# A gated attention scan and a spatial gating unit on one core: a re-timed plan, wider filler matmuls, and the last output tiles in the weight space

## The chip, the cores and the metric

The kernel runs on one core of a Trainium2 chip. The metric is the device time of one execution in microseconds. Five engines work side by side: TensorE (PE in the profile; its weight loads are PEld), VectorE (DVE), ScalarE (ACT), GpSimd (POOL) and SyncE (SP), which here only issues DMAs. Each has its own queue and runs it strictly in order; semaphores tie the queues together.

## The reference, cut to what matters

```python
# q, k, v, alpha: (4, 8, 768, 48)
for t in range(S):                       # S = 768
    state = alpha[:, :, t, :, None] * state + einsum('bhd,bhe->bhde', k[:, :, t], v[:, :, t])
    y[:, :, t] = einsum('bhd,bhde->bhe', q[:, :, t], state)
x = y.transpose(0, 2, 1, 3).reshape(4, 768, 384)
h = maximum(x @ w_in, 0)                 # (4, 768, 1024)
u, v = h[..., :512], h[..., 512:]
v_n = (v - mean(v)) / sqrt(var(v) + 1e-6)
v_s = einsum('ts,bsd->btd', w_spatial, v_n) + b_spatial[None, :, None]
out = (u * v_s) @ w_out                  # (4, 768, 384), float32
```

## The kernel before, in words

**First part, the scan.** Each of the four batches has six chunks of 128 time steps, so there are 24 chunks, 0 to 23. Chunks 0 to 5 go in pairs (`pair`, `PAIRS`), the others singly (`first`). For a chunk, SP loads alpha, k, q and v (`ac`, `kc`, `qc`, `vc`). ACT takes logarithms (`ln`), PE sums them up over time (`cum`), ACT takes exponentials (`einv`, `eexp`, `ebc`). POOL or DVE scales k (`kt`), DVE scales q (`qt`), PE transposes both (`tr`, `trk`), and an evacuation `ev` copies them to `kqT`. PE computes scores (`sc`) into two banks, DVE masks each (`m`, tile `ptm`), and PE forms the chunk's output `y` from the masked scores, v (`vb`) and the state of the chunk before. The state is carried by `upd` (PE), `z` (DVE, L327 and L329), `S` (L334) and `sb` (L209, a copy in two halves into `sbd`). The output is copied (`xs`), transposed (`xt`) and copied into the batch's `xT` (`xe`).

**Second part, per batch.** `second_v` computes the gate half of h for a tile of 128 rows, with its statistics: on DVE (`bn`, L837 and L838), or, for the pairs of tiles named in `ACT_STATS`, on ACT with three small DVE operations `mv` after it. Then come `rs` (ACT) and `vn` (DVE). `second_u` computes the other half, transposed (`uT`). `second_s` multiplies by the spatial weights, adds the bias on DVE (`vsb`, L915) and multiplies by u on POOL (`gT`, L928). `second_o` multiplies by `w_out`, copies a tile of 128 x 384 out of PSUM and stores it. There are 24 such output tiles, numbered n = 6 x batch + row tile. Names such as s-3-0-1 give batch, column slice and row half; o-3-2 is row tile 2 of batch 3.

**The order of work is a plan.** All of this is first written down as operations with a cost on each engine that may run them, with dependencies, a priority and a patience. `schedule` (L96) then places one after the other: at each step the operation and engine with the earliest start, where `PATIENCE` moves the start that is compared, and it emits the instruction. The costs are constants in the code (`ENGINES`, and the numbers in calls of `op`), as are the assumed times of loads (`LD`, and `lat` in `dma`, 1.9 us). The plan so fixes, ahead of time, the order of every engine's queue and on which engine an operation lies. At run time only semaphores decide when an instruction starts.

**Junk matmuls.** While the planned time is below `WARM` = 40 us, `schedule` fills the time for which PE is planned to be idle with matmuls on a constant tile `junk`, in pieces of at most 192 columns. `bank` (L194) emits them, into the bank that the next real operation will overwrite. They do no work of the reference.

**Output tiles.** Where `out_tile` (L935) puts a tile depends on n. Tiles 0 to 7 lie in two tiles of the pool `raws` (`raw_w`, four output tiles each), through which the weights were loaded earlier. Tiles 8 to 10 lie in `w_row`, also of that pool. All the others rotate through four buffers of `outp` (`o_sb`), so that tile n needs the store of tile n - 4 to have landed. The stores stand in SP's queue behind all the loads.

Of the kernel before, what the change touches and what calls it, by code (L numbers as in the profile page):

```python
# [51 lines left out]
class Clock:  # L52
# [19 lines left out]
        return end  # L72


PATIENCE = {"ev": -0.3, "v": -0.1, "g": -0.3, "sb": 0.3, "bb": 0.5, "ln": 0.2, "z": -0.2, "we": -0.1, "S": 0.2, "cast": -0.1, "rs": 0.1, "trk": -0.1, "xs": -0.3}
ENGINES = {
    "kt": {"POOL": 0.87},
    "vb": {"POOL": 0.47, "ACT": 0.42},
    "S": {"POOL": 0.57},
    "sb": {"POOL": 0.79, "DVE": 0.36},  # L80
    "vn": {"DVE": 0.33},
    "xe": {"ACT": 0.38},
    "ev": {"DVE": 0.61, "ACT": 0.91},
    "u": {"ACT": 0.38, "DVE": 0.47},
    "o": {"ACT": 0.38},
}
PAIRS = (0, 1, 2)
ACT_STATS = ((2, 2), (1, 4), (3, 4))
PIECES = {
    "w_in": ((0, "vc", 0, 0.35), (0, "kc", 2, 0.15)),  # L90
    "w_sp": ((0, "vc", 4, 0.35), (0, "qc", 6, 0.25), (0, "qc", 6, 0.25)),
    "w_out": (0, "qc", 7, 0.25),
}
# [2 lines left out]
def schedule(ops, fill, warm_from, warm_to):  # L96

    free = {}
    clock = Clock()
    todo = list(ops)  # L100
    while todo:
        best = None
        for n, op in enumerate(todo):
            if any(d.end is None for d in op.deps):
                continue
            ready = max([d.end + d.lat for d in op.deps], default=0.0)
            waits = [slot.ring.free_at(k) for k, slot in enumerate(op.take)]
            if None in waits:
                continue
            ready = max([ready] + waits)  # L110
            for eng, dur in op.eng.items():
                start = max(ready, free.get(eng, 0.0))
                key = (round(start + (0.5 * dur if len(op.eng) > 1 else 0.0) + op.wait, 2),
                       ready if eng == "DMA" else op.prio)
                if best is None or key < best[0]:
                    best = (key, n, eng, start, dur)
        assert best is not None, "nothing can start"
        _, n, eng, start, dur = best
        op = todo.pop(n)
        if eng == "PE":  # L120
            if op.take and start < warm_to:
                t = max([free.get(eng, 0.0), warm_from] + [slot.ring.free_at(k) for k, slot in enumerate(op.take)])
                while True:
                    each = 0.00042 if clock.warm(t) else 0.00084
                    cols = min(192, int((start - t) / each) // 32 * 32)
                    if cols < 96:
                        break
                    fill.append(cols)
                    t = clock.run(t, 0.00042 * cols, cols)
            end = clock.run(start, dur, op.cols)  # L130
        else:
            end = start + dur
        for slot in op.take:
            slot.ring.taken.append(slot)
        free[eng] = end
        op.end = end
        op.emit(eng)
# [3 lines left out]
def kernel(  # L141
# [31 lines left out]
    IO = 3  # L173
    WK = 3
    NB, NKP = 3, 2
    LD, LP, WT, ST = 0.97, 1.46, 2.35, 0.8
    NRAW, NROW, KEEP = 2, 3, 11
    raws = ctx.enter_context(tc.tile_pool(name="raws", bufs=NRAW))
    io_pool = ctx.enter_context(tc.tile_pool(name="io", bufs=IO))
# [14 lines left out]
    def bank(pool, shape, dtype, **kw):  # L194

        t = pool.tile(shape, dtype, **kw)
        flat = t if len(shape) == 2 else t.rearrange("p a b -> p (a b)")
        for cols in fill:
            nc.tensor.matmul(out=flat[:, 0:cols], lhsT=junk[:, 0:128], rhs=junk[:, 0:cols], start=True, stop=True)  # L199
        fill.clear()  # L200
        return t

# [15 lines left out]
    ut_ones = consts.tile([128, 128], BF16, name="ut_ones")  # L218
    ident = consts.tile([128, 128], BF16, name="ident")
    mask4 = consts.tile([128, 4, 128], BF16, name="mask4")  # L220
    junk = consts.tile([128, 192], BF16, name="junk")
    ones_row = consts.tile([1, 128], BF16, name="ones_row")
    ones_col = consts.tile([128, 1], BF16, name="ones_col")
    eps_tile = consts.tile([128, 1], FP32, name="eps_tile")
# [66 lines left out]
    def op(key, *args, **kw):  # L291

        users = kw.pop("use", ())
        o = Op(*args, **kw)
        for s in users:
            s.users.append(o)
        ops.append(o)
        made[key] = o
        o.wait = PATIENCE.get(key[0], 0.0)
        return o  # L300

    def got(*keys):
        return [made.get(x) for x in keys]
# [86 lines left out]
    def pair(j):  # L390
# [33 lines left out]
        for par in range(2):  # L424
# [42 lines left out]
                    out=ktp[:, par, :, :, 0:D].rearrange("p hp s d -> p (hp s) d"),  # L467
                    in0=st["kc"][:, :, par, :], in1=st[f"binv{par}"])

            op(("ktp", j, par), {"POOL": 0.87, "DVE": 0.47}, None, ktf, got(("einvp", j, par), ("kc", 2 * j)) + tr_users("k", jo), prio=P + 4)  # L470

            def qtf(_, par=par):
                nc.vector.tensor_mul(
# [116 lines left out]
    def first(i):  # L590
# [13 lines left out]

        j = i // 2
        jo = j - NKP
        dma(("ac", i), LD, load("ac", alpha), io_users("ln", j), P)
        dma(("kc", i), LD, load("kc", k), io_users("kt", j), P + 0.1)
        dma(("qc", i), LD, load("qc", q), io_users("qt", j), P + 0.2)
        dma(("vc", i), LD, load("vc", v), io_users("vb", j), P + 0.3)  # L610

        la, kt, qt = [x[j % NKP][:, i % 2].rearrange("p (hp s) d -> p hp s d", s=2) for x in (lap_bufs, ktp_bufs, qtp_bufs)]

# [196 lines left out]
    def second_v(b, tt):  # L810
# [33 lines left out]
        if on_act:  # L844
            def mv(_):
                d = bt[b]
                nc.vector.tensor_scalar_mul(out=d["mvs"][:, two, 0], in0=d["sums"][:, 0, two], scalar1=1.0 / DH)
                nc.vector.tensor_tensor(
                    out=d["mvs"][:, two, 1], in0=d["mvs"][:, two, 0], in1=d["mvs"][:, two, 0], op=ALU.mult)
                nc.vector.scalar_tensor_tensor(  # L850
                    out=d["mvs"][:, two, 1], in0=d["sums"][:, 1, two], scalar=1.0 / DH, in1=d["mvs"][:, two, 1],
                    op0=ALU.mult, op1=ALU.subtract)

            op(("mv", b, t0), "DVE", 0.4, mv, got(("bn", b, t0), ("bn", b, tt)), prio=6.0)

        def rs(_):
            d = bt[b]
# [38 lines left out]
    def second_s(b, dsl, th):  # L896
        last = b == B - 1 and dsl == NDS - 1 and th == 1
        mms = []
        if last:
            mms.append(mm(  # L900
                lambda ps: ps[:, 0:TH], lambda: ones_row, lambda: b_sp_sb[:, th * TH:(th + 1) * TH], True, False))
        for st in range(NT):
            mms.append(mm(
                lambda ps: ps[:, 0:TH], lambda st=st: bt[b]["vn"][:, st, dsl * 128:(dsl + 1) * 128],
                lambda st=st: w_spT[:, st, th * TH:(th + 1) * TH], st == 0 and not last, st == NT - 1))
        hold = {}
        cols = slice(th * TH, (th + 1) * TH)

        def evac(eng, ps):
            if last:  # L910
                nc.vector.tensor_tensor(
                    out=bt[b]["gT"][:, dsl, cols], in0=ps[:, 0:TH], in1=bt[b]["uT"][:, dsl, cols], op=ALU.mult)
            else:
                hold["vs"] = small.tile([128, TH], FP32, name="vsb", bufs=4)
                nc.vector.tensor_tensor(out=hold["vs"], in0=ps[:, 0:TH], in1=bsp_bc[:, th, :], op=ALU.add)  # L915

        Q = 1000.0 + 100 * b + 20 + th * NDS + dsl
        us = got(("u", b, dsl, th))
        pdeps = [[made[("vn", b, t)] for t in tt] for tt in ((0, 1, 2, 3), (4, 5))]
        us = us + got(*[("we", 3 * th + t) for t in range(3)])  # L920
        group(("s", b, dsl, th), mms, 0.165, [made[("v", b, t)] for t in range(NT)] + us,
              Q, evac, "DVE", 0.47,
              us + got(("be", th)) + [made.get(("o", b - 2, x)) for x in range(NT)], parts=2, pdeps=pdeps)
        if last:
            made[("g", b, dsl, th)] = made[("s", b, dsl, th)]
        else:
            def gm(eng):
                ENG[eng].tensor_tensor(  # L928
                    out=bt[b]["gT"][:, dsl, cols], in0=hold["vs"], in1=bt[b]["uT"][:, dsl, cols], op=ALU.mult)

            op(("g", b, dsl, th), {"POOL": 0.87} if b < B - 1 else {"POOL": 0.87, "DVE": 0.46}, None, gm, got(("s", b, dsl, th)), prio=Q)

    kept = {}

    def out_tile(n):  # L935

        if n < 8:
            if n % 4 == 0:
                kept["t"] = raws.tile([128, 4 * DM], FP32, name="raw_w")
            return kept["t"][:, n % 4 * DM:(n % 4 + 1) * DM]  # L940
        if n < KEEP:
            return raws.tile([128, S], BF16, name="w_row", bufs=NROW).bitcast(FP32)
        return outp.tile([128, DM], FP32, name="o_sb")

    def second_o(b, tt):
# [5 lines left out]
        if n < 8:  # L951
            free = [made[("cast", "w_out", x)] for x in range(NDS)] + [made[("cast", "w_sp", 2, x)] for x in range(2)]
        elif n < KEEP:
            free = got(("wt", n - 8 + 3))
        else:
            free = got(("st", (n - 4) // NT, (n - 4) % NT)) if n >= KEEP + 4 else []

        def evac(eng, ps):
            hold["o"] = out_tile(n)
            copy(eng, hold["o"], ps[:, 0:DM])  # L960

        Q = 1000.0 + 100 * b + 30 + tt
        group(("o", b, tt), mms, 0.165, [made[("g", b, x, tt // 3)] for x in range(NDS)] + made[("w_out",)], Q, evac,
# [113 lines left out]
```

## Time and profile before

| | us |
|---|---|
| median of 5 runs | 155.53 |
| lowest, highest | 155.25, 156.05 |
| profiled execution, own time | 155.52 |
| its span, first to last instruction | 153.66 |

The span is 1.9 us shorter than the execution's own time. In the profile, each engine's busy time is given beside its share of the span. "Idle before, releaser" is the time for which an engine stood still just before an instruction, and what ended that. "issue" as a releaser means that nothing that the profile shows was waited for. The bar of a matmul is drawn with the time that it takes to go through the array, so bars of matmuls in sequence overlap; the distance from start to start tells the pace. In strings of digits, each digit is the busy share of one fortieth of the span in tenths.

### The profile page before, as it was taken

Reading aid. Unit: us, or ns where it says so; the run is one execution under the profiler, and the core shown is the slowest. Engines: PE = TensorE matmul, PEld = TensorE weight load, DVE = VectorE, ACT = ScalarE, POOL = GpSimd, SP = SyncE. Lnnn points to the kernel's source line nnn. Section 1 sums busy time; section 2 is a strip of 40 time slices with the busy share of each in tenths; the row PEclk is TensorE's granted clock in tenths of the full one; section 3 lists DMA queues with packets and bytes.
Section 4 is the critical chain, followed back from the end, with each engine's and each line's share of the span. In section 5 each row is a group of like instructions: output and inputs, shape, how many; then the busy total and the mean of one; then the engine's idle time right before and its main releaser. Section 6 shows DMA issues by size and latency. Waiting matters only on the chain.

```text
span 153.7 us, 4564 instructions
## 1 busy us (share of the span) xinstructions
PE 143.7 (94%) x1746; PEld 95.3 (62%) x1761; DVE 123.2 (80%) x268; ACT 111.1 (72%) x273; POOL 84.0 (55%) x141
## 2 busy tenths in 40 slices
PE   7999799999999999999999999999999989999960
PEld 6697567766657556666557575755666646666530
DVE  7666589589999999996888998799979997467900
ACT  3586486899999596899895599999955947860141
POOL 6737247755337888834389498515757851005400
PEclk9999999999999999999999999999999999999998
DMA  4999999998999999989899799899894013400053
GB/s 124 265 314 292 311 211 290 229 281 161 220 232 216 230 182 203 201 164 211 161 215 205 151 201 212 162 216 220 192 376 171 2 51 107 154 0 0 2 196 117
DMA packets 93016, 28.62 MB, mean 186 GB/s; under 512 B 87873, under 2 KB 91457, under 8 KB 92993
## 3 DMA queue, kind: packets, MB, share of 16 engines
q1 hardware_dynamic: 92960, 28.32, 78.4%
q8 instruction: 14, 0.23, 0.7%
q14 instruction: 10, 0.07, 0.1%
q0 software_dynamic: 32, 0.00, 0.0%
HBM read 23.60 MB, written 4.72 MB: 184 GB/s over the span
## 4 chain that ended last, share of the span: by engine, by line
PE 74%; ACT 8%; DVE 5%; DMA 5%; POOL 2%; issue 2%; ACTq 0%; DVEq 0%; POOLq 0%
PE ps L775 41%; PE pt L672 4%; PE pt L702 4%; DMA out_dram<-o_sb 3%; PE y L363 3%; DMA ac<-in_alpha_dram 2%; PE y L730 2%; PE cum L621 2%; PE tp L688 2%; PE y L573 2%; PE ps L199 2%; POOL gT L928 2%; PE ps L430 2%; PE y L724 2%; PE ps L495 2%
## 5 line engine op out<-in xcount | busy, mean ns | idle before, releaser
L775 PE MATMUL ps<-w_spT,vn 128*128 128x384 bf16 x192 | 36.2, 326 | 0.0
L928 POOL TENSOR_TENSOR gT<-vsb,uT 128x384 bf16<-128x384 f32 x28 | 25.8, 930 | 17.3 <-DVE vsb L915 16.9
L713 DVE TENSOR_TENSOR ptm<-pt,mask 128x512 bf16<-128x512 f32 x36 | 23.5, 682 | 2.0 <-PE pt L702 1.8
L775 PEld LDWEIGHTS <-vn 128*128 128x128 bf16 x192 | 17.1, 97 | 10.2 <-issue 0.2
L645 POOL TENSOR_TENSOR kt<-kc,binv 128x384 bf16<-128x384 f32 x18 | 16.5, 920 | 10.5 <-ACT bc L640 5.5
L334 POOL TENSOR_TENSOR state<-state,bc 128x192 f32<-128x192 f32 x20 | 10.3, 513 | 20.3 <-DVE state L329 12.6
L775 PE MATMUL ps<-w_out_sb,gT 128*128 128x384 bf16 x96 | 18.6, 326 | 0.0
L775 PE MATMUL ps<-xT,w_in 128*128 128x384 bf16 x96 | 18.4, 326 | 0.0
L207 ACT CAST x_sb<-y 128x384 bf16<-128x384 f32 x24 | 11.4, 480 | 9.2 <-PE y L730 6.4
L915 DVE TENSOR_TENSOR vsb<-ps,bsp_bc 128x384 f32<-128x384 f32 x31 | 16.3, 550 | 2.1 <-PE ps L775 1.2
L775 PE MATMUL ps<-w_in,xT 128*128 128x512 bf16 x57 | 16.1, 380 | 1.2 <-ACT xT L207 0.2
L207 ACT COPY o_sb<-ps 128x384 f32<-128x384 f32 x13 | 6.2, 476 | 11.3 <-PE ps L775 9.7
L837 DVE BATCH_NORM_STATS2 stats<-v_sb 128x6 f32<-128x512 bf16 x18 | 12.3, 685 | 1.5 <-ACT v_sb L213 1.4
L213 ACT ACTIVATE v_sb<-ps 128x512 bf16<-128x512 f32 x18 | 10.7, 596 | 3.8 <-PE ps L775 3.4
L207 ACT COPY xT<-y 128x384 bf16<-128x384 bf16 x24 | 11.4, 486 | 1.4 <-PE y L363 1.1
L209 POOL CAST sbd<-state 64x192 bf16<-64x192 f32 x30 | 11.2, 374 | 1.3
L199 PEld LDWEIGHTS <-junk 128*128 128x128 bf16 x112 | 10.4, 108 | 2.0 <-DVE junk L240 1.1
L775 PEld LDWEIGHTS <-gT 128*128 128x128 bf16 x96 | 8.4, 97 | 5.0
L775 PEld LDWEIGHTS <-w_in 128*128 128x128 bf16 x96 | 8.4, 97 | 4.9
L215 DVE TENSOR_SCALAR uT<-ps 128x384 bf16<-128x384 f32 x16 | 8.5, 553 | 3.4 <-PE ps L775 3.3
L867 DVE TENSOR_SCALAR vn<-v_sb,mvs,rstd 128x512 bf16<-128x512 bf16 x24 | 10.5, 473 | 0.8 <-ACT rstd L860 0.7
L775 PEld LDWEIGHTS <-xT 128*128 128x128 bf16 x72 | 6.1, 98 | 6.8 <-ACT xT L207 2.4
(128 smaller groups left out, 314.2 us busy)
## 6 DMA issues: line engine op xcount, KB each, us to landing
ac<-in_alpha_dram SPq DMA_DIRECT2D x18, 192.0 KB, 4.1
kc<-in_k_dram SPq DMA_DIRECT2D x18, 192.0 KB, 4.1
qc<-in_q_dram SPq DMA_DIRECT2D x18, 192.0 KB, 3.7
vc<-in_v_dram SPq DMA_DIRECT2D x18, 192.0 KB, 4.1
out_dram<-o_sb SPq DMA_DIRECT2D x13, 192.0 KB, 2.1
raw_w<-in_moe_w_spatial_dram SPq DMA_DIRECT2D x3, 768.0 KB, 6.2
raw_w<-in_moe_w_in_dram SPq DMA_DIRECT2D x2, 768.0 KB, 8.2
out_dram<-raw_w SPq DMA_DIRECT2D x8, 192.0 KB, 2.5
```

Source lines behind the costliest of these rows:

```text
L199: nc.tensor.matmul(out=flat[:, 0:cols], lhsT=junk[:, 0:128], rhs=junk[:, 0:cols], start=True, stop=True)
L207: nc.scalar.copy(out=out, in_=in_)
L209: ENG[eng].tensor_copy(out=out, in_=in_)
L213: nc.scalar.activation(out=out, in_=in_, func=AF.Relu)
L334: ENG[eng].tensor_tensor(out=st["state"], in0=st["state"], in1=st["bc"][:, :, None].to_broadcast([128, HP, D]), op=ALU.mult)
L645: ENG[eng].tensor_mul(out=kt[:, :, :, 0:D], in0=quad(st["kc"]), in1=st["binv"])
L713: nc.vector.tensor_tensor(out=st["ptm"][:, s], in0=st[f"pt{s}"], in1=mask4, op=ALU.mult)
L775: return lambda ps: nc.tensor.matmul(out=out(ps), lhsT=lhsT(), rhs=rhs(), start=start, stop=stop)
L837: nc.vector.bn_stats(out=stats, in_=d["v_sb"][:, tt, :])
L867: nc.vector.tensor_scalar(out=d["vn"][:, t, :], in0=d["v_sb"][:, t, :], scalar1=d["mvs"][:, t, 0:1], scalar2=d["rstd"][:, t:t + 1], op0=AL ...
L915: nc.vector.tensor_tensor(out=hold["vs"], in0=ps[:, 0:TH], in1=bsp_bc[:, th, :], op=ALU.add)
L928: ENG[eng].tensor_tensor(out=bt[b]["gT"][:, dsl, cols], in0=hold["vs"], in1=bt[b]["uT"][:, dsl, cols], op=ALU.mult)
```

## The change

Five things change at once.

- The planner's constants: costs in `ENGINES` and in some calls of `op`, patience, and an assumed load latency `LATE` = 3.5 us for the chunks 6 to 23 in place of 1.9. `S` and `sb` may both run on POOL or DVE. `ACT_STATS` has two pairs of tiles in place of three. One of the two `w_in` loads is tied to the load of v of the second chunk in place of the first, which leaves its place in the queue as it was.
- A table `NUDGE` of 21 single operations, each with a shift of its patience.
- Junk matmuls of up to 384 columns in place of 192, cut to the width of the bank that they are written to; the tile `junk` is 384 columns wide.
- The last four output tiles, n = 20 to 23, lie in one more `raw_w` tile in place of `o_sb`. They depend on the stores of tiles 0 to 3.
- The copy of tile 23 out of PSUM is split in two halves, one on ACT and one on DVE.

With the new constants, the planner gives every engine another order from early on. PE's first 24 groups stay as they are; after that, the first part's chunks 6 to 8 come later among the second part's work. `NUDGE` puts o-3-2 behind o-3-3, o-3-4 and o-3-5 at the very end.

```diff
-PATIENCE = {"ev": -0.3, "v": -0.1, "g": -0.3, "sb": 0.3, "bb": 0.5, "ln": 0.2, "z": -0.2, "we": -0.1, "S": 0.2, "cast": -0.1, "rs": 0.1, "trk": -0.1, "xs": -0.3}
+PATIENCE = {"ev": -0.3, "kt": -0.2, "v": -0.1, "be": 0.2, "sb": 0.3, "bb": 0.2, "ln": 0.2, "z": -0.2, "we": -0.1, "S": 0.2, "cast": -0.1, "rs": 0.1, "trk": -0.1, "xs": -0.3, "xe": -0.2, "y": -0.2}
 ENGINES = {
-    "kt": {"POOL": 0.87},
-    "vb": {"POOL": 0.47, "ACT": 0.42},
-    "S": {"POOL": 0.57},
-    "sb": {"POOL": 0.79, "DVE": 0.36},
-    "vn": {"DVE": 0.33},
-    "xe": {"ACT": 0.38},
+    "kt": {"POOL": 0.9},
+    "vb": {"POOL": 0.48, "ACT": 0.42},
+    "S": {"POOL": 0.5, "DVE": 0.6},
+    "sb": {"POOL": 0.73, "DVE": 0.95},
+    "vn": {"DVE": 0.42},
+    "xe": {"ACT": 0.4},
     "ev": {"DVE": 0.61, "ACT": 0.91},
-    "u": {"ACT": 0.38, "DVE": 0.47},
-    "o": {"ACT": 0.38},
+    "u": {"ACT": 0.39, "DVE": 0.49},
+    "o": {"ACT": 0.4},
+}
+NUDGE = {
+    ("m", 9, 0): -0.15,
+    ("vn", 0, 4): -0.3,
...
+    ("ebc", 0): 0.15,
...
+    ("kc", 0): 1,
+    ("o", 3, 2, "mm", 0): 0.3,
...
 }
 PAIRS = (0, 1, 2)
-ACT_STATS = ((2, 2), (1, 4), (3, 4))
+LATE = 3.5
+ACT_STATS = ((2, 2), (0, 2))
 PIECES = {
-    "w_in": ((0, "vc", 0, 0.35), (0, "kc", 2, 0.15)),
+    "w_in": ((0, "vc", 1, 0.35), (0, "kc", 2, 0.15)),
...
-                    cols = min(192, int((start - t) / each) // 32 * 32)
+                    cols = min(384, int((start - t) / each) // 32 * 32)
...
-    LD, LP, WT, ST = 0.97, 1.46, 2.35, 0.8
+    LD, LP, WT, ST = 1.03, 1.46, 2.35, 0.8
...
         for cols in fill:
-            nc.tensor.matmul(out=flat[:, 0:cols], lhsT=junk[:, 0:128], rhs=junk[:, 0:cols], start=True, stop=True)
+            for c in range(0, cols, flat.shape[1]):
+                n = min(cols - c, flat.shape[1])
+                nc.tensor.matmul(out=flat[:, 0:n], lhsT=junk[:, 0:128], rhs=junk[:, 0:n], start=True, stop=True)
...
-    junk = consts.tile([128, 192], BF16, name="junk")
+    junk = consts.tile([128, 384], BF16, name="junk")
...
-        o.wait = PATIENCE.get(key[0], 0.0)
+        o.wait = PATIENCE.get(key[0], 0.0) + NUDGE.get(key, 0.0)
...
-        dma(("ac", i), LD, load("ac", alpha), io_users("ln", j), P)
+        dma(("ac", i), LD, load("ac", alpha), io_users("ln", j), P, lat=LATE)
...
-            op(("mv", b, t0), "DVE", 0.4, mv, got(("bn", b, t0), ("bn", b, tt)), prio=6.0)
+            op(("mv", b, t0), "DVE", 0.9, mv, got(("bn", b, t0), ("bn", b, tt)), prio=6.0)
...
-            op(("g", b, dsl, th), {"POOL": 0.87} if b < B - 1 else {"POOL": 0.87, "DVE": 0.46}, None, gm, got(("s", b, dsl, th)), prio=Q)
+            op(("g", b, dsl, th), {"POOL": 0.9} if b < B - 1 else {"POOL": 0.9, "DVE": 0.69}, None, gm, got(("s", b, dsl, th)), prio=Q)
...
-        if n < 8:
+        if n < 8 or n >= B * NT - 4:
...
+        elif n >= B * NT - 4:
+            free = got(*[("st", 0, x) for x in range(4)])
...
             hold["o"] = out_tile(n)
-            copy(eng, hold["o"], ps[:, 0:DM])
+            if n < B * NT - 1:
+                copy(eng, hold["o"], ps[:, 0:DM])
+                return
+            half = DM // 2
+            copy("ACT", hold["o"][:, 0:half], ps[:, 0:half])
+            copy("DVE", hold["o"][:, half:DM], ps[:, half:DM])
```

The loads of k, q and v of chunks 6 to 23 get `lat=LATE` in the same way, and the cost of `ktp` goes from 0.87 and 0.47 to 0.9 and 0.6.

More of the change, by code (lines that the diff above doesn't have):

```diff
@@ L72, in run @@
         return end
-PATIENCE = {"ev": -0.3, "v": -0.1, "g": -0.3, "sb": 0.3, "bb": 0.5, "ln": 0.2, "z": -0.2, "we": -0.1, "S": 0.2, "cast": -0.1, "rs": 0.1, "trk": -0.1, "xs": -0.3}
+PATIENCE = {"ev": -0.3, "kt": -0.2, "v": -0.1, "be": 0.2, "sb": 0.3, "bb": 0.2, "ln": 0.2, "z": -0.2, "we": -0.1, "S": 0.2, "cast": -0.1, "rs": 0.1, "trk": -0.1, "xs": -0.3, "xe": -0.2, "y": -0.2}
 ENGINES = {
-    "kt": {"POOL": 0.87},
-    "vb": {"POOL": 0.47, "ACT": 0.42},
-    "S": {"POOL": 0.57},
-    "sb": {"POOL": 0.79, "DVE": 0.36},
-    "vn": {"DVE": 0.33},
-    "xe": {"ACT": 0.38},
-    "ev": {"DVE": 0.61, "ACT": 0.91},
-    "u": {"ACT": 0.38, "DVE": 0.47},
-    "o": {"ACT": 0.38},
+    "kt": {"POOL": 0.9},
[4 more added lines that the diff above has]
+    "xe": {"ACT": 0.4},
+    "ev": {"DVE": 0.61, "ACT": 0.91},
+    "u": {"ACT": 0.39, "DVE": 0.49},
[4 more added lines that the diff above has]
+    ("vn", 0, 4): -0.3,
+    ("qt", 22): -0.3,
+    ("upd", 2): 0.3,
+    ("v", 0, 5): 0.6,
+    ("vbp", 0, 0): -0.6,
+    ("z", 21): 1.5,
+    ("ebc", 0): 0.15,
+    ("ev", "q", 1, 1): 0.15,
+    ("z", 19): -1.5,
+    ("cast", "w_in", 0, 1): -0.15,
+    ("vb", 21): -0.15,
+    ("y", 19): -1.5,
+    ("kc", 0): 1,
+    ("o", 3, 2, "mm", 0): 0.3,
+    ("sc", 1, 0): -0.3,
+    ("tr", "k", 0, 1): -0.3,
+    ("qtp", 0, 0): -0.15,
+    ("y", 2): 0.15,
+    ("xs", 22): -0.3,
+    ("m", 20, 0): 0.6,
 }
 PAIRS = (0, 1, 2)
-ACT_STATS = ((2, 2), (1, 4), (3, 4))
+LATE = 3.5
+ACT_STATS = ((2, 2), (0, 2))
 PIECES = {
-    "w_in": ((0, "vc", 0, 0.35), (0, "kc", 2, 0.15)),
+    "w_in": ((0, "vc", 1, 0.35), (0, "kc", 2, 0.15)),
     "w_sp": ((0, "vc", 4, 0.35), (0, "qc", 6, 0.25), (0, "qc", 6, 0.25)),
@@ L468, in ktf @@
                     in0=st["kc"][:, :, par, :], in1=st[f"binv{par}"])
-            op(("ktp", j, par), {"POOL": 0.87, "DVE": 0.47}, None, ktf, got(("einvp", j, par), ("kc", 2 * j)) + tr_users("k", jo), prio=P + 4)
+            op(("ktp", j, par), {"POOL": 0.9, "DVE": 0.6}, None, ktf, got(("einvp", j, par), ("kc", 2 * j)) + tr_users("k", jo), prio=P + 4)
             def qtf(_, par=par):
@@ L606, in first @@
         jo = j - NKP
-        dma(("ac", i), LD, load("ac", alpha), io_users("ln", j), P)
-        dma(("kc", i), LD, load("kc", k), io_users("kt", j), P + 0.1)
-        dma(("qc", i), LD, load("qc", q), io_users("qt", j), P + 0.2)
-        dma(("vc", i), LD, load("vc", v), io_users("vb", j), P + 0.3)
+        dma(("ac", i), LD, load("ac", alpha), io_users("ln", j), P, lat=LATE)
+        dma(("kc", i), LD, load("kc", k), io_users("kt", j), P + 0.1, lat=LATE)
+        dma(("qc", i), LD, load("qc", q), io_users("qt", j), P + 0.2, lat=LATE)
+        dma(("vc", i), LD, load("vc", v), io_users("vb", j), P + 0.3, lat=LATE)
         la, kt, qt = [x[j % NKP][:, i % 2].rearrange("p (hp s) d -> p hp s d", s=2) for x in (lap_bufs, ktp_bufs, qtp_bufs)]
```

## The prediction

> **What bounds the kernel now.** I read the page's first two parts, then TensorE's idle times, then the chain at the end. The busy shares:
>
> ```profile
> PE 143.7 (94%) x1746; PEld 95.3 (62%) x1761; DVE 123.2 (80%) x268; ACT 111.1 (72%) x273; POOL 84.0 (55%) x141
> ...
> PE   7999799999999999999999999999999989999960
> ```
>
> TensorE (PE) is the bound from 2 us to 148.6 us; nobody else is at nine tenths for so long. But not all of it is work: line L199 is junk, put in to fill idle time that the planner foresees. From start to start a junk matmul of 192 columns takes 83 ns, one real matmul of 384 columns 162 ns. The order of PE's instructions has 112 junk matmuls, 20,896 columns; 4,544 of them run before the first real matmul, while the first load is on its way, and cost nothing. The other 16,352 are 16,352/192 x 83 ns = 7.1 us, all before 39 us. Junk is executed whether PE is late or not, so **what delays PE early on is not made up by it**. A PE delay therefore reaches the end, unless another engine is later still.
>
> Second, what PE waited for:
>
> ```profile
> PE y L573 <- issue: 1.0, 1, 1.0
> PE y L724 <- DVE sbd L209: 0.7, 1, 0.7
> ```
>
> (us in total, times, longest), and at these two places of the timeline (start, us, then in brackets the idle time and its releaser):
>
> ```profile
> 16.94 0.27 PE L573 MATMUL y<-vbp,ptm 64*128 64x48 bf16 x4 [1.01 <-issue]
> ...
> 123.91 0.34 PE L724 MATMUL y<-sbd,kqT 128*128 128x96 bf16 x4 [0.66 <-DVE sbd L209]
> ```
>
> A matmul's bar reaches past the start of the next one, so I count waits from start to start, less the usual pitch. Above 0.25 us and after 5 us that gives: 1.17 us at 15.7 (in the middle of one y, waiting for no engine), 0.46 at 34.8 (chunk 6's transposes `trk`, behind masks on VectorE), 0.39 at 74.6 (v, behind ACT's xT), 0.28 at 78.0 (scores, behind ACT's kqT copy of 1.02 us), 0.83 at 122.9 (y, behind two state copies on DVE, 0.47 and 0.40 us). In all 3.1 us: more can't be got back in the middle.
>
> The first belongs to this row of part 3:
>
> ```profile
> q8 instruction: 14, 0.23, 0.7%
> ```
>
> 14 packets, 0.23 MB, so 16 KB each: PE's instructions (its 3,524 matmuls and weight loads alone are about 14 x 256). One starts at 14.31 us and lasts 1.23 us, among loads that keep the DMA engines full. PE stops after its 452nd matmul or weight load at 15.7 us and goes on at 16.94.
>
> Third, the end:
>
> ```profile
> 145.18 3.41 PE L775 MATMUL ps<-w_out_sb,gT 128*128 128x384 bf16 x20
> ...
> 147.33 0.48 ACT L207 COPY o_sb<-ps 128x384 f32<-128x384 f32 x1 [0.17 <-PE ps L775]
> 149.43 0.94 ACT L207 COPY o_sb<-ps 128x384 f32<-128x384 f32 x2 [1.62 <-DMA out_dram<-o_sb]
> ```
>
> PE is done at 148.59, yet the last two copies wait for a store that frees their buffer: `outp` has four. The last store is issued at 150.40, SP sees the last landing at 152.55, and closing takes 1.1 us, to 153.66.
>
> **What the Trainium skill says.** Runtime: NRT & Kernel Launch, "Instruction fetch mechanics": instructions are refilled in 16 KiB blocks of 256, over DMA, while the current block executes, "mostly hidden". The trace agrees on the size, and shows one block that was not hidden (1.0 us). TensorE: Matmul & The Clock Gate, "Back-to-back issue gap": warm pitch N/2.4 + 2.5 ns, so 162.5 for 384 columns and 82.5 for 192; the trace has 162 and 83. The same page, "What's actually happening": half the clock until about 3.4 us of activity. The first 24 junk matmuls take 3.97 us, 165 ns each, later ones 83. DMA: Bandwidth & Descriptors, "Latency and other measured facts": about 2 us fixed per DMA; stores of o_sb land after 1.8 to 3.9 us, median 2.1.
>
> **The change, part by part.**
>
> *Wider junk.* 71 matmuls in place of 112, 22,752 columns, of which 4,544 are again the free ones. The rest, 18,208, at 162/384 to 83/192 ns a column, are 7.7 to 7.9 us: **+0.7 us** on PE. The extra sits before y-4 (1,376 columns) and v-0-4 (640). If PE would have waited there anyway the price is 0; the full 0.85 us of those two is the other end.
>
> Each piece less is one matmul and one weight load less. PE reaches its 452nd such instruction not at y-1 but ten groups on, where before stood at about 20 us; the 256 instructions up to there take some 8 us in place of 5.5. A block that came 1.2 us late then has 3 us to spare. **-1.0 us**, from 0 (the chains of DVE and ACT take it) to -1.2. I don't take all, as the planner still writes 0.38 to 0.40 us for ACT copies that take 0.48.
>
> The junk tile's memset doubles (0.22 us now); its cover is the 0.3 us that PE then waits for the first logarithm anyway: 0.
>
> *Plan.* New costs, patience and nudges change the order on every queue; arithmetic and loads are the same. Work moves: five state copies `sb` (2 x 0.364 us each on DVE) and seven uT (0.553) leave DVE, one on-ACT statistics pair (1.73 on DVE, less 0.78 for its three small operations) comes, three S (0.35 by the nearest row, the state sum L329; at most the 0.51 that POOL takes), two kqT copies (1.1) come, one kt, one w_spT go: DVE -3.6 -3.9 +1.0 +1.05 +1.1 -1.1 + 0.3 (half a copy) = about -5 us, to 118. ACT -2.1 +3.4 -1.6 -1.0 with small ones: about -1, to 110. POOL +3.7 (sb, 0.75 each) -1.5 +0.9 +1.0 +0.5 = about +4.6, to 89. PE's sum doesn't change. Of the waits, 122.9 goes (its sb is on POOL), 78.0 goes (that copy is on DVE, 0.68 for 1.02), 34.8 goes (trk-6 is twelve groups later): **-1.6 us**. 74.6 stays. POOL's cover is its 45% idle; without it, each sb 0.75 us long would hold up the next y.
>
> The plan takes 3.5 us for a load's latency where 1.9 stood, so chunks 6 to 13 come later, while loads keep SP's order but for a few exchanges: the buffers that they wait for come free later. Loads were ahead of their use by 4 us at chunk 6, which covers that.
>
> What is late next: the masks. A y needs its scores' two masks: 0.16 + 1.28 + 0.06 = 1.5 us after the last score matmul if DVE is free. Adding up PE durations in the new order, the distance is 1.5 to 2.0 us for chunks 7, 10 to 13, 22 and 23, where before only 7 and 8 had less than 2. With one DVE operation of 0.55 ahead of the masks in each, y's would wait 2.2 us in all; with none, 0. I take half. Besides, o-3-2 is nudged to the very end, so only o-3-1 covers the last gT (0.56 us on DVE): 0.25 us. **+1.35 us**, from 0.25 to 2.5.
>
> *Tiles.* The last four output tiles get one `raw_w` tile, whose readers, the first stores, were issued from 115 us on. No copy waits for a store. PE's end aside, the last copy (o-3-2, whole, 0.48 on ACT) ends at 148.59 + 0.04 + 0.48 = 149.11, against 150.37: **-1.25 us**. The halved copy of tile 23 is last but one and wins nothing. Five of the last six SP issues take 0.33 to 0.62 us, one 1.14, so SP is free by then; landing is taken at 2.1. If four stores in flight slow the last to 3.9, it ends 0.5 us later than now; if 1.8, another 0.3 is won.
>
> Sum: 0.7 - 1.0 - 1.6 + 1.35 - 1.25 = -1.8 us. The profiled execution took 155.52 us (span 153.66), the median of the five is 155.53: **153.7 us**.
>
> **Rivals.**
> 1. *The middle gives nothing*: what the fetch and the waits free is lost to DVE and ACT, whose chains run through the same 40 us. For it: DVE is at nine tenths in most slices from 30 us on, ACT in many. Against: DVE loses 5 us of work. Junk +0.7, tail -1.25: 155.0.
> 2. *Late masks make it slower*: the place is y of chunks 7 to 13 and 18 to 23, the price what DVE holds before the masks. With 0.8 us there, they wait 4.5 us: 0.7 - 1.0 - 1.6 + 4.7 - 1.25 = +1.55, 157.1. It decides from about 0.7 us. Against: the same 0.8 would have cost y's 1.3 us before, and none of its waits of 0.15 or more is at those y's but the one behind sbd.
> 3. *The tail's gain is eaten by landing*: 3.9 us, as one store showed at 145.4. -1.8 + 1.25 + 0.5: 155.5.
>
> **How the numbers follow.** The forecast has 0.64, rival 1 0.16, rival 2 0.13, rival 3 0.07. Best ends of the unknown terms (+0.7 - 1.2 - 1.6 + 0.25 - 1.5) give 152.2, worst short of rival 2 about 155.5. Range 152.0 to 155.5; rival 2 lies outside. About 0.3%, 0.47 us, is what a measurement can tell here. Faster by more: nearly all of the forecast, most of rival 1: 0.76; within: the rest and rival 3: 0.10; slower: 0.14.
>
> **What would show it.** Right: no "issue" wait of a y near 16 us; no o_sb or raw_w copy waiting for a DMA at the end; DVE near 118 busy; span near 151.9; PE's last matmul within a microsecond of 148. Wrong: waits of y for ptm of over 3 us; a 16 KB fetch with a PE gap behind it; last landing over 3 us after its issue.

## The result, and the profile after

| | before | after |
|---|---|---|
| median of all runs, us | 155.39 (154.45 to 157.05) | 154.89 (154.77 to 155.21) |
| ratio | 1 | 0.997, 95% interval 0.9961 to 0.9979 |
| profiled execution, own time | 155.52 | 154.98 |
| its span | 153.66 | 153.21 |
| PE's last matmul ends | 148.59 | 148.61 |
| last copy out of PSUM ends | 150.37 | 149.13 |
| last store issued | 150.40 | 149.16 |
| SP sees its landing | 152.56 | 152.10 |

The change gives 0.5 us, where 1.8 was forecast. Ratios, here and below, leave out executions over 1.5% slower than the fastest of their kernel, which the medians of all runs include. The profile page after, its busy shares and PE's slices, and its rows of instruction packets (queue, packets, MB, share of 16 DMA engines):

```profile
PE 144.8 (95%) x1702; PEld 91.8 (60%) x1720; DVE 119.5 (78%) x256; ACT 111.9 (73%) x270; POOL 87.8 (57%) x152
...
PE   6999999998999999999999999999999999999970
...
q8 instruction: 13, 0.21, 0.6%
q14 instruction: 8, 0.07, 0.2%
```

PE has 1.1 us more to do (wider junk) and one block of 16 KB less to fetch. The loads of the engines came out as worked out: DVE 119.5 for 118, ACT 111.9 for 110, POOL 87.8 for 89. What PE waited for (us in total, times, longest):

```profile
PE y L389 <- ACT x_sb L233: 0.4, 1, 0.4
PE ps L801 <- issue: 0.4, 2, 0.2
PE ps L801 <- ACT xT L233: 0.2, 1, 0.2
PE y L750 <- POOL gT L954: 0.2, 1, 0.2
PE pt L728 <- DVE kqT L235: 0.2, 1, 0.2
```

The pause of a y behind "issue" is gone, and so is the y behind `sbd`; the two "issue" places of 0.2 us are no pauses: at both (97.4 and 104.6 us) the record of the matmul just before is missing from the trace, while its weight load is there. The timeline where the pause was (start, us, group):

```profile
15.20 0.89 PE L599 MATMUL y<-vbp,ptm 64*128 64x48 bf16 x32
16.03 0.34 PE L605 MATMUL y<-sbd,kqT 128*128 128x96 bf16 x4
```

All 32 matmuls follow each other. At 28.8 us PE is 1.08 us ahead of before; at 148.6 it is level. And the end:

```profile
145.20 3.41 PE L801 MATMUL ps<-w_out_sb,gT 128*128 128x384 bf16 x20
...
147.20 2.34 SPq L1000 DMA_DIRECT2D out_dram<-raw_w  x4
...
148.00 0.32 ACT L233 COPY raw_w<-ps 128x192 f32<-128x192 f32 x1 [0.17 <-PE ps L801]
148.35 0.36 DVE L235 COPY raw_w<-ps 128x192 f32<-128x192 f32 x1 [2.32 <-ACT raw_w L233]
148.65 0.48 ACT L233 COPY raw_w<-ps 128x384 f32<-128x384 f32 x1 [0.33 <-PE ps L801]
```

No copy waits for a DMA, as predicted, and the last ends at 149.13 (149.11 was worked out). But then SP waits longer, as its waits say:

```profile
SPq L1105 <- DMA out_dram<-raw_w: 2.5, 1, 2.5
```

Before, the corresponding row read

```profile
SPq L1072 <- DMA out_dram<-o_sb: 1.5, 1, 1.5
```

From issue to landing the last store took 2.94 us, before 2.16.

### The profile page after: what moved, and what is told of

Read it like the earlier page. It is cut to its first block, busy times and chain, and to the rows that moved or that the text cites. A ratio compares the mean times of both kernels' runs of the same rounds, so it can differ in the third digit from the quotient of the medians.

```text
span 153.2 us, 4470 instructions
## 1 busy us (share of the span) xinstructions
PE 144.8 (95%) x1702; PEld 91.8 (60%) x1720; DVE 119.5 (78%) x256; ACT 111.9 (73%) x270; POOL 87.8 (57%) x152
## 4 chain that ended last, share of the span: by engine, by line
PE 87%; ACT 4%; issue 2%; DVE 2%; POOL 1%
PE ps L801 47%; PE pt L698 6%; PE ps L225 5%; PE pt L728 3%; PE y L389 3%; PE cum L647 2%; PE y L756 2%; PE tp L714 2%; PE ps L456 2%; PE y L599 2%; PE y L750 2%; PE ps L521 2%; PE ps L811 2%; PE y L225 2%; PE pt L572 1%
## 5 line engine op out<-in xcount | busy, mean ns | idle before, releaser
L863 DVE BATCH_NORM_STATS2 stats<-v_sb 128x6 f32<-128x512 bf16 x20 | 13.7, 686 | 5.3 <-ACT v_sb L239 5.1
L801 PE MATMUL ps<-w_in,xT 128*128 128x512 bf16 x54 | 15.3, 380 | 1.4 <-issue 0.4
L239 ACT ACTIVATE v_sb<-ps 128x512 bf16<-128x512 f32 x20 | 11.9, 597 | 6.0 <-PE ps L801 5.1
L360 POOL TENSOR_TENSOR state<-state,bc 128x192 f32<-128x192 f32 x17 | 8.7, 514 | 11.3 <-DVE state L353 7.3
L235 POOL CAST sbd<-state 64x192 bf16<-64x192 f32 x40 | 13.8, 346 | 2.3 <-DVE state L360 0.6
L893 DVE TENSOR_SCALAR vn<-v_sb,mvs,rstd 128x512 bf16<-128x512 bf16 x24 | 11.7, 518 | 0.2
L233 ACT COPY o_sb<-ps 128x384 f32<-128x384 f32 x9 | 4.3, 483 | 9.9 <-PE ps L801 9.9
L239 ACT ACTIVATE uT<-ps 128x384 bf16<-128x384 f32 x23 | 10.7, 488 | 0.4 <-PE ps L801 0.4
L681 DVE TENSOR_TENSOR qt<-qc,cum 128x384 bf16<-128x384 f32 x18 | 9.8, 549 | 0.8 <-ACT cum L676 0.6
L659 ACT ACTIVATE binv<-cum 128x384 bf16<-128x384 f32 x18 | 8.7, 493 | 2.2 <-POOL sbd L235 0.7
```

The source lines that it names most:

```text
L233: nc.scalar.copy(out=out, in_=in_)
L235: ENG[eng].tensor_copy(out=out, in_=in_)
L239: nc.scalar.activation(out=out, in_=in_, func=AF.Relu)
L681: nc.vector.tensor_mul(out=qt[:, :, :, 0:D], in0=quad(st["qc"]), in1=st["cv"])
L801: return lambda ps: nc.tensor.matmul(out=out(ps), lhsT=lhsT(), rhs=rhs(), start=start, stop=stop)
L863: nc.vector.bn_stats(out=stats, in_=d["v_sb"][:, tt, :])
```

## The experiments

Each kernel starts from the kernel before (names with b) or after (names with a), with the edit shown. They were timed in four groups, each on one chip together with the kernel before: b_wide, b_tail, b_wide_tail and a_warm32; a_192, a_again, a_o32 and b_wide_pad96; a_o32_warm32, a_whole, a_notail and b_wide_tail_sb; a_pad8 and a_dve. Ratios are to the kernel before in the same group; its median was 155.89, 155.29, 155.20 and 155.15 us. Medians of different groups compare less safely than those of one.

### The fetch pause: wide junk alone, tile change alone, both, and narrow junk in the new plan

**b_wide**, before with wide junk and nothing else:

```diff
-cols = min(192, int((start - t) / each) // 32 * 32)
+cols = min(384, int((start - t) / each) // 32 * 32)
...
-nc.tensor.matmul(out=flat[:, 0:cols], lhsT=junk[:, 0:128], rhs=junk[:, 0:cols], start=True, stop=True)
+for c in range(0, cols, flat.shape[1]):
+    n = min(cols - c, flat.shape[1])
+    nc.tensor.matmul(out=flat[:, 0:n], lhsT=junk[:, 0:128], rhs=junk[:, 0:n], start=True, stop=True)
...
-junk = consts.tile([128, 192], BF16, name="junk")
+junk = consts.tile([128, 384], BF16, name="junk")
```

> The kernel before with junk matmuls of up to 384 columns and nothing else: every queue keeps its order, junk is 20,960 columns in 60 planned pieces in place of 20,896 in 112. Theory A (the pause of 1.2 us in a y at 15.7 us is a late block of instructions, and a delay of TensorE so early reaches the end): the pause is gone and the kernel is 1.0 to 1.2 us faster, about 154.3. Theory B (the early time is lost again to VectorE's and ScalarE's chains, whatever the plan): the pause is gone, but the end moves by less than 0.4 us, about 155.2. Theory C (the pause is not the fetch): the pause stays.

153.44 us, ratio 0.9858 (0.9817 to 0.9899).

**b_tail**, before with the tile change and the halved copy of tile 23 alone:

```diff
-if n < 8:
+if n < 8 or n >= B * NT - 4:
...
+elif n >= B * NT - 4:
+    free = got(*[("st", 0, x) for x in range(4)])
...
-copy(eng, hold["o"], ps[:, 0:DM])
+if n < B * NT - 1:
+    copy(eng, hold["o"], ps[:, 0:DM])
+    return
...
+copy("ACT", hold["o"][:, 0:half], ps[:, 0:half])
+copy("DVE", hold["o"][:, half:DM], ps[:, half:DM])
```

> The kernel before with the last four output tiles in one raw_w tile and the last copy out of PSUM halved, nothing else. The prediction's step: 1.25 us faster, as the last store is issued so much earlier (about 154.2). Theory of the landing: the stores of the last tiles share the DMA engines, so an earlier issue waits longer for its landing; 0.4 to 0.6 us faster (about 154.9), with the last landing 2.7 us or more after its issue.

154.66 us, ratio 0.9938 (0.9911 to 0.9966).

**b_wide_tail**, both of these edits.

> Wide junk and the tile change together on the order of the kernel before; only the new plan is missing. If both parts add up as predicted: 2.3 us faster (153.1). With theory A and the theory of the landing: 1.6 us faster (153.8), and then the new plan itself costs about 1.1 us. With theory B and the landing: 0.5 us faster (154.9), like the changed kernel, and the plan costs nothing.

153.48 us, ratio 0.9857 (0.9810 to 0.9904).

**a_192**, after with junk of 192 columns; **a_again**, after unchanged, in the same group:

```diff
-cols = min(384, int((start - t) / each) // 32 * 32)
+cols = min(192, int((start - t) / each) // 32 * 32)
```

> The changed kernel with junk of at most 192 columns again; all orders stay, TensorE has 96 instructions more. Theory of the instruction blocks: the pause near 16 us comes back (0.8 to 1.2 us), there is a 14th block again, fetched during the last stores, so 1.0 to 2 us slower than the changed kernel (about 156.3). If the pause belonged to the old order alone: no change within 0.2 us.

> The changed kernel once more, as the control of this group: 0.3% faster than before if the first comparison holds on this chip. The best variant so far, wide junk alone on the old order, was 1.4% faster than before; if the new plan costs as much as that suggests, the changed kernel is 1.2 to 1.6 us behind it on any chip.

156.06 us, ratio 1.0062 (1.0045 to 1.0079), against 154.83 us, 0.9963 (0.9948 to 0.9978). In the timeline of a_192 the pause is back, two matmuls before the end of the same y:

```profile
15.08 0.84 PE L599 MATMUL y<-vbp,ptm 64*128 64x48 bf16 x30
16.96 0.22 PE L599 MATMUL y<-vbp,ptm 64*128 64x48 bf16 x2 [1.03 <-issue]
```

What follows. The pause of about 1.2 us comes with narrow junk (before, b_tail, a_192) and goes with wide junk (b_wide, b_wide_tail, after), in either plan. The kernel's description above says that at run time only semaphores decide when an instruction starts; this pause is an exception: PE waited for no semaphore, and fewer PE instructions ahead of it take the pause away. On the new plan that is worth 1.23 us, and PE's last matmul starts at 149.33 in a_192 against 148.28. (a_192 has a 14th block again, but not during the last stores, as was expected: it comes at 145.71, 0.75 us before the next store is issued, and that store has no late part.) On the old plan wide junk alone brings 1.4%, about 2.2 us and over four times what the whole change brings, and the tile change adds nothing to it, though alone it brings 0.6%. Both take away the same loss at the end. The trace records a landing for each of 16 parts of a store. For the store that the copies of before wait for:

| | issued | PE's last 16 KB block | 15 of 16 parts landed | last part |
|---|---|---|---|---|
| before | 145.40 | 146.34, for 1.61 us | 147.25 | 149.33 |
| b_tail | 145.54 | 146.62, for 1.14 us | 147.38 | 149.10 |
| b_wide | 145.32 | none | 147.14 | 147.16 |

Fifteen parts land as always, one is 1.7 to 2.1 us late, and only in the two kernels whose PE fetches its 14th block just then. The new plan shows the same 14 us earlier: in seven kernels (after, a_again, a_o32, a_whole, a_notail, a_pad8, a_dve) PE's 13th block starts at 132.0 to 132.3 us, and the two stores issued at 131.2 to 132.1 us each have one part 1.2 to 2.1 us late; in a_warm32 and a_o32_warm32 the block comes at 133.2 and 132.9 us, and no part is late. Before, the last two copies queued behind that one part. With 13 blocks (wide junk) it is not late, and four buffers are nearly enough: in b_wide the copies end at 149.07. The profiled execution of b_wide was the slowest of its six (154.09 us): PE lost 0.8 us at 84 us behind ScalarE's xT, so there it ends no earlier than before (148.51 against 148.59), and what that trace wins is the tail alone.

**b_wide_pad96** was to bring the 14th block back without the early pause: wide junk up to 15 us, at most 96 columns later.

```diff
-cols = min(192, int((start - t) / each) // 32 * 32)
+cols = min(384 if start < 15.0 else 96, int((start - t) / each) // 32 * 32)
```

> The kernel before with junk of up to 384 columns for what is planned before 15 us and of at most 96 after it: the early instruction count falls as with wide junk, the whole count (3,518) is again that of before (3,524). Theory of two effects: the pause near 16 us is gone (1.1 us won), but the 14th block is fetched in the last stores' time again, their landing is late and the copies wait for a buffer (1.2 us not won), so about 1.1 us faster than before in place of 2.4. If wide junk won all of its 2.4 us by the pause alone: 2.4 us faster here too.

153.29 us, ratio 0.9877 (0.9851 to 0.9903). The 14th block came, but only at 151.95 us, after the stores, so the run says nothing on a late block at the end; that a late block holds up a store rests on the comparison of kernels above. No cost of more and smaller junk after 15 us is seen. The trace also shows what the early pause is worth on the old plan: PE's last matmul starts at 147.33 in place of 148.27, so 0.9 of the 2.2 us. The rest is the tail's.

### What eats the gain: late junk, the nudge of o-3-2, the halved copy, the tiles

**a_warm32**, after with `WARM` at 32 us, which leaves out the two late fills (2,016 columns, before y-4 and v-0-4):

```diff
-    WARM = 40.0
+    WARM = 32.0
```

> The changed kernel with junk only while the planned time is below 32 us: the two fills ahead of y-4 and v-0-4, 2,016 columns or 0.85 us, are left out, all orders stay. If they delay TensorE as junk does that nobody needs: 0.85 us faster than the changed kernel, about 154.0. If TensorE would have waited there for the masks and copies anyway: no change, 154.9, with waits of 0.6 and 0.3 us in their place.

154.63 us, ratio 0.9940 (0.9918 to 0.9963); a_again in another group has 0.9963, so the ratios hardly tell the two apart. In the traces PE's last matmul starts at 147.88 in place of 148.28, 0.4 us earlier, not 0.85, and 0.16 of this is there at 9 us, long before the fills. Without them PE waits for others: at 33.7 us 0.38 longer, for masks, and at 36.3 us about as long as the second fill took. So 0.2 to 0.4 us of the late junk is paid for, half of it at most.

**a_o32**, after without the nudge of o-3-2, and **a_o32_warm32**, with `WARM` at 32 besides:

```diff
-    ("o", 3, 2, "mm", 0): 0.3,
```

> The changed kernel without the nudge that puts o-3-2 last: TensorE ends with o-3-2, o-3-3, o-3-4, o-3-5, so that two groups cover the last gT and the halved copy is the last. If the order of the last stores costs the late landing (2.9 us after the last issue, against 1.9 with the same tile change on the old order): 0.5 to 1.0 us faster than the changed kernel. If the late landing comes from where an instruction block of another engine falls: no more than 0.15 us.

> The changed kernel without the o-3-2 nudge and without the two late fills of junk. If the two costs are separate and add up: 0.75 us (nudge) and 0.25 to 0.4 us (fills) faster than the changed kernel, about 153.7. If the fills only hide waits that the shorter tail would show again: no faster than without the nudge alone, 154.1.

154.06 us, ratio 0.9928 (0.9902 to 0.9953), and 153.66 us, 0.9920 (0.9895 to 0.9945). Between these two, of different groups, the last store is issued 0.43 us earlier (148.88 for 149.31), the medians differ by 0.4 us, the ratios by 0.1%: the upper end of what the late junk costs. The first is 0.77 us under a_again in its own group, and **its reason is not the one that it looks like**: the last store is issued at 149.31, later than after's 149.16, and still lands 0.9 us earlier.

**a_whole**, after with tile 23 copied whole (by ScalarE), the nudge kept:

```diff
-if n < B * NT - 1:
+if n < B * NT:
     copy(eng, hold["o"], ps[:, 0:DM])
     return
```

> The changed kernel with tile 23 copied whole on ScalarE; the nudge stays, o-3-2 is last. The last two stores are then issued some 0.65 us apart, not 0.42. If the late last landing comes from two stores close together: the landing takes 2.2 us or less, 0.5 us or more faster than the changed kernel (154.3). If it comes from the 8 KB instruction packet that falls behind the last issue: with the packet still there the landing stays near 2.9 us (154.9 to 155.0); with the packet gone from there it takes 1.9 (about 154.0).

153.82 us, ratio 0.9925 (0.9902 to 0.9948): by the medians 1.0 us faster than after (by the ratios 0.6 to 0.7; the changed kernel was timed in other groups), with the nudge in place. The copies end at 148.97, only 0.16 us earlier; the rest is the landing, 1.89 us after the issue.

**a_notail**, after with the last four tiles in `o_sb`, copied whole:

```diff
-if n < 8 or n >= B * NT - 4:
+if n < 8:
...
-elif n >= B * NT - 4:
-    free = got(*[("st", 0, x) for x in range(4)])
...
-if n < B * NT - 1:
+if n < B * NT:
```

> The changed kernel with its last four output tiles in o_sb again and tile 23 copied whole, everything else as it is but the order of the last three copies and stores. The prediction's step: 1.25 us slower (156.1). If wide junk alone has cured the tail already (13 instruction blocks, so that the first of the last stores lands in 2 us and its buffer is free in time): within 0.3 us of the changed kernel, or faster, if o-3-2 is no longer the last copy.

155.34 us, ratio 1.0022 (1.0003 to 1.0041), 1.5 us over a_whole in the same group. The fourth of the last copies runs at 148.71, 1.95 us after the third began: of the stores before it, the one issued at 146.62 has landed just then, at 148.49. So with this plan the tiles are needed.

### Why the last store lands late

At this point three causes stood for the 1.0 us: a packet of instructions (queue q14, 8 KB) among the last store's packets, the small distance (0.42 us) of the last two issues, or two engines writing one tile. Two more runs separate them.

**a_pad8**, after with eight tiny memsets on VectorE, at about 6 us, where it waits for its first `kt`:

```diff
+    pad = consts.tile([128, 8], BF16, name="pad")
...
                 nc.vector.memset(eps_tile, LN_EPS)
+                for x in range(8):
+                    nc.vector.memset(pad[:, x:x + 1], 0.0)
```

> The changed kernel, with eight more memsets of one column on VectorE, of a tile that nobody reads, put at about 6 us, where VectorE waits for its first kt; nothing else differs, and the order on the other engines is the same. It shifts VectorE's instruction numbers by eight. Theory A (an 8 KB packet of instructions falls among the last store's packets, because the halved copy gives VectorE one instruction more at the end): the packet at 150.4 us comes earlier, before 149 us, the last store lands in 1.9 us instead of 2.9, and the time falls by 0.9 to 1.0 to about 153.9 us. Theory B (the landing is slow because the last two stores are issued only 0.42 us apart, or because two engines write the last tile): nothing changes, 154.8 us.

153.91 us, ratio 0.9911 (0.9878 to 0.9945). **a_dve**, after with tile 23 copied whole by VectorE:

```diff
-copy("ACT", hold["o"][:, 0:half], ps[:, 0:half])
-copy("DVE", hold["o"][:, half:DM], ps[:, half:DM])
+copy("DVE", hold["o"], ps[:, 0:DM])
```

> The changed kernel, with tile 23 copied whole by VectorE instead of in two halves; ScalarE loses its half, VectorE has as many instructions as with the halves. Theory A (the packet of instructions): it still falls at about 150.4 to 150.6 us and the landing stays at 2.9, so 154.8 us, although whole copying by ScalarE gave 153.8. Theory B (two engines writing one tile): the landing is 1.9 and the time 153.8 to 154.0 us. If it is the distance of the last two issues (about 0.3 us here, if the whole copy on VectorE takes 0.5): 154.8 or more, and then only the run with the memsets tells the two apart.

154.80 us, ratio 0.9973 (0.9957 to 0.9989). Here is the DMA view of after from 149.2 to 152.6 us, the stretch of the last store (busy share of the 16 DMA engines in 40 slices, 85 ns each; then the queues; then KB and us to landing):

```profile
DMA  5000499999999999720001010000000000000000
...
q14 instruction: 1, 0.01, 0.8%
...
out_dram<-raw_w SPq DMA_DIRECT2D x1, 192.0 KB, 2.9
```

And the same stretch of a_pad8, in which the queue q14 has no row:

```profile
DMA  1003999999999989300000000000000000000000
...
q1 hardware_dynamic: 300, 0.40, 33.0%
...
out_dram<-raw_w SPq DMA_DIRECT2D x1, 192.0 KB, 2.0
```

In both, the bulk of the store goes through in some 14 slices. In after, eight single packets of 1.5 KB follow one by one until 151.61: 12 KB, one part of 16. The first of them starts at 150.86, just as the 8 KB packet ends (150.42 and 0.44 us). That is how it would look if the DMA engine that carries this part had the 8 KB packet first; the trace does not name the engine of a packet. The wait of SP in a_pad8:

```profile
SPq L1108 <- DMA out_dram<-raw_w: 1.5, 1, 1.5
```

Kernels side by side, from the trace's packets and landings (us):

| | last issue | last 8 KB packet, of any engine | 15 of 16 parts landed | last part |
|---|---|---|---|---|
| before | 150.40 | 150.42 | 152.51 | 152.53 |
| after | 149.16 | 150.42 | 151.12 | 152.08 |
| a_again | 149.28 | 150.56 | 151.24 | 152.17 |
| a_192 | 150.20 | 151.49 | 152.16 | 153.09 |
| a_warm32 | 148.75 | 150.01 | 150.71 | 151.61 |
| a_dve | 149.22 | 150.25 | 151.09 | 151.91 |
| a_pad8 | 149.08 | 143.93 | 151.02 | 151.05 |
| a_o32 | 149.31 | 146.84 | 151.13 | 151.16 |
| a_whole | 149.00 | 152.66 | 150.84 | 150.87 |
| b_wide | 149.10 | 149.37 | 150.95 | 151.19 |
| b_wide_tail | 148.81 | 146.72 | 150.63 | 150.65 |

What follows. Where the packet comes 1.0 to 1.3 us after the issue, the last part lands 0.8 to 1.0 us after the others, and the store 2.7 to 2.9 us after its issue. Where it comes before the issue or after the landing, all 16 parts land together, after 1.8 to 2.0. In b_wide, with the packet 0.27 us after the issue, one part loses a quarter of a microsecond; in before, with 0.02 us, none does. a_pad8 leaves the halves, the two writers and the 0.42 us between the last issues as they were, and is 0.9 us faster than a_dve in the same group, and than after, by eight memsets that compute nothing: that takes out both other causes. a_dve takes the second writer away and keeps VectorE's count of instructions, and stays slow. Eight VectorE instructions move the packet, so it belongs to VectorE's stream. In all five slow kernels it comes 1.6 to 1.7 us after VectorE's last copy ends (148.71 in after, 148.62 in a_dve), and without that copy, in a_whole, it comes only after the landing. The halved copy did the harm by giving VectorE one instruction more at the end. In before and b_wide VectorE's work ends by 146.0, so the packets at 150.42 and 149.37 are probably another engine's. In a_o32 the packet came at 146.84; there the trace has one VectorE record more (323 for 322), a second semaphore wait at 145.5 us, ahead of the last copy. So its gain goes with the packet's place, too.

### A version that beats both

**b_wide_tail_sb**: the old plan with wide junk and the new tiles, and one cost changed, so that the planner puts state copies on POOL:

```diff
-    "sb": {"POOL": 0.79, "DVE": 0.36},
+    "sb": {"POOL": 0.75, "DVE": 0.95},
```

> The old order with wide junk and the tile change, and of the new plan's costs only the one for the state copy sb (0.95 us on VectorE, 0.75 on GpSimd, for 0.36 and 0.79): four of the five copies leave VectorE, and TensorE's order stays but for some groups around y-21 to y-23. The wait of 0.83 us at 122 us behind the two copies goes: 0.5 to 0.8 us faster than the same kernel without it (153.48), about 152.8, the fastest here. If GpSimd is then late with them: no faster than 153.4.

152.17 us (152.06 to 152.31), ratio 0.9819 (0.9796 to 0.9842), against 0.997 for after and, in the same group, 153.82 us for a_whole. The chain at 122 us shows why. b_wide_tail has, as before,

```profile
123.36 0.34 PE L726 MATMUL y<-sbd,kqT 128*128 128x96 bf16 x4 [0.66 <-DVE sbd L211]
```

and b_wide_tail_sb has no wait there:

```profile
122.87 0.66 PE L777 MATMUL ps<-w_spT,vn 128*128 128x384 bf16 x3
123.37 0.33 PE L726 MATMUL y<-sbd,kqT 128*128 128x96 bf16 x4
```

That wait was 0.82 us from start to start; PE's last matmul starts at 146.51, 1.2 us earlier than in b_wide_tail, but 0.3 of this is there by 6 us, before any of these copies. (By the medians of two groups it is 1.3 us faster than b_wide_tail, by the ratios 0.6.) Compared with it, a_pad8 and a_whole, which have the whole new plan and no packet in the way, take 153.9 and 153.8 us: what the new plan wins at 122 us it gives back elsewhere.

## Why the prediction was wrong

The forecast of 153.7 us missed by 1.2: it was right in direction and the gain far too large. Two steps failed: the landing of the last store, taken as 2.1 us with the halved copy priced at nothing, and the new waits of PE, taken as 1.35 us. Step by step:

- **Fetch pause, -1.0: right, a little small.** It went, and a_192 puts it at 1.23 us. At 28.8 us PE had 1.08.
- **Wider junk, +0.7: too dear, and the wrong thing was counted.** The two late fills take their 0.85 us, but a_warm32 and a_o32_warm32 show that PE would wait for half of it or more without them: the price is 0.2 to 0.4. What the step missed is that fewer pieces of junk also take away the 14th block, whose fetch at 146 us held up a store. In the kernel before, that is most of the loss at the tail, so on the old plan wide junk alone brought 2.2 us.
- **Plan, waits removed, -1.6: right.** 34.8, 78.0 and 122.9 are gone (0.46 + 0.28 + 0.83 = 1.57 us); 0.39 behind xT stays, now at 66.9. (Of this, in both kernels, 0.2 us is a matmul whose record is missing: the wait itself is 0.2.)
- **Plan, new waits, +1.35: mis-sized and misplaced.** PE ends where it ended before, 148.61 for 148.59, against -0.55 in the forecast. With the late junk as executed, 0.85 us, 0.85 - 1.17 - 1.57 leaves it 1.89 us ahead, so new waits of 1.91 us took that back. From start to start, those above 0.25 us are 0.57 at 35.9 (xT's transposes behind ACT's x_sb), 0.37 at 53.2 (y behind gT), 0.36 at 90.3 (scores behind DVE's kqT) and 0.29 at 101.6 (y): 1.59 us, the rest is in smaller pieces. None is a y behind its masks. The step looked for the danger at one place and the planner had moved it to four others.
- **Tiles, -1.25: the copies right, the landing wrong.** The copies end 1.24 us earlier. "The halved copy of tile 23 is last but one and wins nothing" priced it at 0, and "landing is taken at 2.1" followed. It cost VectorE one instruction, and so 0.9 to 1.0 us (a_pad8, a_whole against a_again). The step won 0.46 us.

The two failed terms are 0.6 us (new waits) and 0.8 (landing), together a little more than the miss. Without the packet the same change takes 153.8 to 153.9 us (a_whole, a_pad8), close to the forecast, but partly by luck: PE ends no more than 0.15 us earlier than before there, for the 0.55 of the forecast, and the store lands after 1.9 to 2.0 us, in place of 2.1.

Of the rivals, the first gave the time, 155.0, and half of its reason: the middle gave nothing. But it put its whole tail gain at 1.25, and the trace shows 0.46; and the time went to new waits of PE. The two largest measured behind ACT and DVE are 0.57 and 0.36 us, so a part of this rival's reason may hold; whether these engines were full just there was not looked into. The second, late masks, did not happen. The third, a late landing, did, at 2.9 rather than 3.9 us; the prediction gave it 0.07 and blamed four stores in flight, where it was one packet of instructions. The trace of the kernel before had shown the like: a store that lands after 3.9 us, and a 16 KB packet that starts at 146.34 while it is on its way. It was read as a spread of landings.

The Trainium skill, Runtime: NRT & Kernel Launch, "Instruction fetch mechanics", calls the fetch "mostly hidden". For the engine that fetches, that is true here but for one block in fourteen. For the stores the traces differ: a store that a fetch meets has one part that is up to 2.1 us late. Its blocks of 16 KiB are what PE fetches here; the packets of the other queue, VectorE's among them, have 8 KB.

What stays open: why a packet costs a store nothing when it comes with the issue (before), 0.25 us at 0.3 us after it (b_wide), and most at 1.0 to 1.3 us; why the first block that PE fetches is late and the others are not; and which of the 21 nudges and costs make the new waits.

## What to carry to other kernels

Count instructions at the end as well as time: here the fetch of a block that no engine waited for delayed the one store that ends the kernel. Before blaming a slow last landing on the stores, look at the instruction packets in its stretch, and shift the stream by a few idle instructions to test it. And take a plan apart: three edits, picked by testing parts of the change, gave 1.8% here where all of it together gave 0.3%.

## What the runs showed of the hardware that was not expected

- Instruction packets and stores get in each other's way. An 8 KB packet (0.31 to 0.44 us long) that comes a microsecond after the issue of a store goes with one of its 16 parts landing 0.8 to 1.0 us late (five kernels); a 16 KB one (1.0 to 1.8 us) that starts 0.1 to 1.1 us after the issue with 1.2 to 2.1 us (nine kernels).
- Eight memsets of one column, placed in idle time over 140 us ahead of the end, made a kernel of 154.8 us 0.9 us faster.
- Fewer, wider matmuls with the same or more columns took away a pause and a late fetch at once: 71 junk matmuls (68 in b_wide) in place of 112 saved one block out of 14.
